# One prefix-sum matmul per unit instead of two, with exps of both signs and r divided by w, in a new order of instructions

## The chip, the cores and the metric

The kernel runs on one core of a Trainium2 chip. Its time is the device time of one execution in microseconds (us). Each run of a changed kernel is timed beside the kernel before on the same chip. A ratio is the mean time of one kernel's fast runs over the mean of the other's fast runs of the same rounds, so it is not quite the ratio of the medians that I quote; the brackets behind it are its 95% interval. One per cent is 2.2 us here. A single profiled execution can be a microsecond off its kernel's median, so I take verdicts from ratios and read mechanisms from profiles.

## The reference

An RWKV-style recurrence over 4 x 768 tokens with 8 heads of 48 gives x; a gated MLP of width 1536 follows.

```python
for t in range(S):                                  # recurrence, per batch and head
    cur = einsum('bhd,bhe->bhde', u * kt, vt)
    y[:, :, t] = einsum('bhd,bhde->bhe', rt, state + cur)
    state = wt[..., None] * state + einsum('bhd,bhe->bhde', kt, vt)
xn = x / sqrt(mean(x * x) + 1e-6) * rms_g           # then the MLP on 3072 tokens
g = xn @ w_gate
out = (g * sigmoid(g) * (xn @ w_val)) @ w_out
```

## The kernel before

The tokens are cut into six super-blocks (SB0 to SB5) of 128 steps, each with four units, one per batch. A unit (m, j) needs the decay up to each step: prefix sums of ln w over the 128 steps, their exp, and r and k multiplied by it. One sum must include the step itself and the other must not, so the kernel before makes two sums with two masks, each in its own PSUM bank, and takes one exp over both banks:

```python
def cs_mm(self, m, j):                              # TensorE: the prefix sums
    ps = self.b2(("cs", m, j))                      # a pair of the 8 PSUM banks
    rhs = self.lw[:, self.slot["lw", m], j, :, 0:D]
    for i, mask in ((0, self.mask_nge), (1, self.mask_gt)):
        if i or m not in ONE_SUM:                   # ONE_SUM = () before
            self.nc.tensor.matmul(ps[:, i, 0:DM]..., lhsT=mask, rhs=rhs, start=True, stop=True)

def cs_exp(self, m, j):                             # ScalarE: in place, in the banks
    ps = self.b2(("cs", m, j))[:, :, 0:DM]
    if m in ONE_SUM:
        self.nc.scalar.activation(out=ps[:, 0], in_=ps[:, 1], func=AF.Exp, scale=-1.0)
        self.nc.scalar.activation(out=ps[:, 1], in_=ps[:, 1], func=AF.Exp)
    else:
        self.nc.scalar.activation(out=ps, in_=ps, func=AF.Exp)

def rk_mul(self, m, j):                             # VectorE: the decay product
    self.nc.vector.tensor_tensor(out=self.rkA[...], in0=self.in_rk[:, self.slot["in_rk", m], j],
                                 in1=ps_of_unit, op=ALU.mult)      # (cut) frees the bank pair
```

I call `rk_mul` the decay product. It is the last reader of the pair of banks, so until it has run no matmul can write there. That makes a chain for each super-block: ln, sums, exp, decay product, and only then the next use of those two banks, which may be another unit's sum or a gate matmul of the MLP.

All instructions are issued in an order written as a list of steps, with the engine where there is a choice (`A` ScalarE, `V` VectorE, `G` GpSimd) and after `@` the bank or the semaphore group:

```
ln.3.0.4   ln w of SB3        cs.3.1  sums of unit 1     exp.3.1  their exp     rk.3.1  decay product
ruk1.3.1   r*k on GpSimd      xn.2.1/V  normalise a tile of x     gv.2.0.3.g  gate matmul of the MLP
```

## Time and profile before

| | |
|---|---|
| time | 217.6 us median of three (216.13 to 219.59) |
| TensorE busy | 194.1 of 216.3 us, 90% |
| first gate matmul of SB0 / SB1 / SB2 | 32.91 / 66.92 / 103.35 us |
| end | 216.3 us |

The first gate matmul of a super-block's MLP is a good milestone, as the recurrence of that block must be done by then. The lines themselves are shown in the prediction.

### The profile page before, as it was taken

How to read it: one execution, taken by the hardware profiler on the slowest of the kernel's cores; microseconds unless marked ns; L12 is line 12 of the kernel's file. 1: busy time of each engine (PE TensorE's matmuls, PEld its weight loads, DVE VectorE, ACT ScalarE, POOL GpSimd, SP SyncE). 2: the span in 40 equal slices, each digit the busy share in tenths (PEclk: the TensorE clock that was granted, in tenths of full speed). 3: DMA queues.
4: the chain of work that ended last, by engine and by line, in shares of the span. 5: the costliest groups of instructions: out<-in, count | busy, mean ns of one | idle time of the engine just before them, and what ended most of it. 6: DMA issues, size and time to landing. Idle time of an engine off the chain costs nothing.

```text
span 216.3 us, 4472 instructions
## 1 busy us (share of the span) xinstructions
PE 194.1 (90%) x1660; PEld 119.0 (55%) x1660; DVE 151.8 (70%) x244; ACT 128.1 (59%) x232; POOL 111.4 (52%) x139
## 2 busy tenths in 40 slices
PE   1257999999899999886999999999999999999992
PEld 0035547887577868663345555455564555544451
DVE  2039678084999989989779969798968995226530
ACT  3355895668967896586434777637986426034401
POOL 3277895058766969495951662776966012000000
PEclk9999999999999999999699999999999999999999
DMA  6999979999999899999999798999557512221013
GB/s 138 185 213 260 364 258 295 314 189 217 188 220 196 180 179 228 141 207 148 220 195 209 142 240 171 165 211 223 128 124 161 41 54 41 65 99 72 5 36 109
DMA packets 130774, 36.94 MB, mean 171 GB/s; under 512 B 124480, under 2 KB 129216, under 8 KB 130752
## 3 DMA queue, kind: packets, MB, share of 16 engines
q1 hardware_dynamic: 130352, 36.65, 78.8%
q8 instruction: 13, 0.21, 0.4%
q14 instruction: 9, 0.07, 0.2%
q10 hardware_dynamic: 400, 0.00, 0.1%
HBM read 26.15 MB, written 4.72 MB: 143 GB/s over the span
## 4 chain that ended last, share of the span: by engine, by line
PE 67%; SPq 8%; POOL 8%; DMA 5%; issue 4%; ACT 4%; DVE 2%; ACTq 0%; POOLq 0%; DVEq 0%
PE ps L511 37%; PE ps L527 16%; SPq L290 7%; PE ps L498 4%; PE ps L411 2%; PE ps L370 2%; DMA rkT<-rkA 2%; PE ps L427 2%; DMA xnt<-xnr 2%; POOL st L446 1%; POOL ydr L464 1%; PE ps L399 1%; POOL ruk L452 1%; DVE rkA L386 1%; PE ps L424 1%
## 5 line engine op out<-in xcount | busy, mean ns | idle before, releaser
L515 ACT ACTIVATE sg<-ps 128x512 bf16<-128x512 f32 x72 | 41.4, 596 | 37.4 <-PE ps L511 30.3
L519 DVE TENSOR_TENSOR ht<-ps,sg 128x512 bf16<-128x512 f32 x72 | 48.0, 685 | 18.4 <-PE ps L511 12.1
L511 PE MATMUL ps<-xnt,wg 128*128 128x256 bf16 (+1 forms) x288 | 56.3, 330 | 0.9 <-DVE xnt L335 0.5
L511 PE MATMUL ps<-xnt,wv 128*128 128x256 bf16 (+1 forms) x288 | 55.7, 329 | 0.0
L527 PE MATMUL ps<-wo,ht 128*128 128x384 bf16 x288 | 53.5, 326 | 0.0
L511 PEld LDWEIGHTS <-wv 128*128 128x128 bf16 x288 | 27.9, 99 | 18.2 <-issue 1.4
L527 PEld LDWEIGHTS <-ht 128*128 128x128 bf16 x288 | 27.3, 98 | 18.0 <-DVE ht L519 0.2
L452 POOL TENSOR_TENSOR ruk<-in_rk 128x384 f32<-128x384 f32 x24 | 24.6, 1028 | 23.5 <-DMA in_rk<-in_r_dram 13.5
L511 PEld LDWEIGHTS <-wg 128*128 128x128 bf16 x288 | 27.1, 98 | 17.2 <-issue 1.9
L414 DVE TENSOR_TENSOR qts<-ps,mask_lt 128x1024 bf16<-128x1024 f32 x24 | 28.7, 1217 | 2.0 <-PE ps L411 1.9
L477 POOL TENSOR_TENSOR rstd<-rstd,mhalf 128x1 f32<-128x1 f32 x24 | 13.5, 565 | 26.9 <-ACT junk L472 26.8
L386 DVE TENSOR_TENSOR rkA<-in_rk,ps 128x768 bf16<-128x768 f32 x24 | 22.5, 949 | 5.7 <-ACT wcr L363 2.2
L456 POOL TENSOR_TENSOR ruk<-ruk,u_bc 128x384 f32<-128x384 f32 x24 | 24.4, 1023 | 2.0 <-DMA u_bc<-in_u_dram 1.3
L379 ACT ACTIVATE ps<-ps 128x768 f32<-128x768 f32 x24 | 18.6, 795 | 9.0 <-PE ps L370 8.4
L464 POOL TENSOR_TENSOR ydr<-in_v,diag 128x384 f32<-128x384 f32 x24 | 20.3, 850 | 4.3 <-DVE diag L459 4.2
L472 ACT ACTIVATE junk<-xb 128x388 bf16<-128x388 bf16 x24 | 12.6, 524 | 12.9 <-DVE xb L468 12.8
L370 PE MATMUL ps<-lw,mask_nge 128*128 128x384 bf16 x24 | 8.5, 354 | 11.3 <-ACT lw L329 8.4
L459 DVE TENSOR_REDUCE diag<-ruk 128x8 f32<-128x384 f32 x24 | 13.0, 544 | 4.4 <-POOL ruk L456 4.4
L326 ACT ACT_TABLE_LOAD x12 | 15.4, 1283 | 0.9 <-PEq L571 0.7
L446 POOL TENSOR_TENSOR st<-sf,wcr 128x384 bf16<-128x384 f32 x17 | 14.0, 828 | 2.3 <-ACT wcr L363 2.2
L339 ACT COPY obr<-ps 128x384 f32<-128x384 f32 x14 | 6.6, 478 | 12.6 <-PE ps L527 12.4
L468 DVE TENSOR_TENSOR xb<-ps,ydr 128x384 bf16<-128x384 f32 x24 | 12.9, 549 | 1.6 <-PE ps L427 1.6
(71 smaller groups left out, 201.8 us busy)
## 6 DMA issues: line engine op xcount, KB each, us to landing
in_w<-in_w_dram SPq DMA_DIRECT2D x24, 192.0 KB, 3.7
in_rk<-in_k_dram SPq DMA_DIRECT2D x24, 192.0 KB, 3.8
in_rk<-in_r_dram SPq DMA_DIRECT2D x24, 192.0 KB, 4.1
in_v<-in_v_dram SPq DMA_DIRECT2D x24, 192.0 KB, 3.9
out_dram<-obr SPq DMA_DIRECT2D x24, 192.0 KB, 2.1
ht<-in_moe_w_val_dram SPq DMA_DIRECT2D x4, 384.0 KB, 4.3
ht<-in_moe_w_out_dram SPq DMA_DIRECT2D x4, 384.0 KB, 6.3
ht<-in_moe_w_gate_dram SPq DMA_DIRECT2D x3, 384.0 KB, 8.2
```

The lines of the kernel that those rows point to most:

```text
L326: self.nc.scalar.preload_act_table_set(LN_EXP if kind == "le" else SILU)
L379: self.nc.scalar.activation(out=ps, in_=ps, func=AF.Exp)
L386: self.nc.vector.tensor_tensor(out=self.rkA[:, self.slot["rkA", m, j], :, :, 0:D], in0=self.in_rk[:, self.slot["in_rk", m], j], in1=self.b ...
L414: self.nc.vector.tensor_tensor(out=self.qts[:, self.slot["qts", m, j]].rearrange("p a q t -> p (a q) t"), in0=self.b2(("qb", m, j)).rearra ...
L446: (self.nc.vector if eng == "DVE" else self.nc.gpsimd).tensor_tensor(out=self.st[:, m % 2, j].rearrange("p q (a d) -> p q a d", a=2), in0= ...
L452: self.nc.gpsimd.tensor_tensor(out=self.ruk[:, self.slot["ruk", m, j]], in0=rk[:, 0], in1=rk[:, 1], op=ALU.mult)
L456: self.nc.gpsimd.tensor_tensor(out=t, in0=t, in1=self.u_bc, op=ALU.mult)
L464: self.nc.gpsimd.tensor_tensor(out=self.ydr[:, self.slot["ydr", m, j]], in0=self.in_v[:, self.slot["in_v", m], j], in1=self.diag[:, m * SB ...
L511: self.nc.tensor.matmul(ps[:, a * n:(a + 1) * n], lhsT=w[:, c, f * 128:(f + 1) * 128], rhs=x[:, c], start=(a == 0 and c == 0), stop=(a == ...
L515: self.nc.scalar.activation(out=self.sg[:, self.slot["sg", m, g, i]], in_=self.b1(("gvb", m, g, i, "g")), func=AF.Silu)
L519: self.nc.vector.tensor_tensor(out=self.ht[:, self.slot["ht", m], fs[0]:fs[-1] + 1, t0:t0 + n], in0=self.b1(("gvb", m, g, i, "v")).rearran ...
L527: self.nc.tensor.matmul(ps, lhsT=self.ht[:, self.slot["ht", m], f, j * L:(j + 1) * L], rhs=self.wo[:, f, :], start=(f == 0), stop=(f == FC ...
```

## The change

The intent is to take one of the two prefix-sum matmuls away in the 16 units of SB2 to SB5. One sum stays, and its exp is taken with both signs. What the second sum had more, the step's own ln w, is put back by multiplying r with exp(-ln w). The order of instructions was then searched anew, and it differs nearly everywhere.

```diff
-ONE_SUM = ()
+ONE_SUM = (2, 3, 4, 5)
+    def inv_w(self, m):                    # ScalarE, once per super-block: 1/w = exp(-ln w)
+        self.nc.scalar.activation(out=self.iw[...], in_=self.lw[...], func=AF.Exp, scale=-1.0)
-    def r_over_w(self, m, j):              # was there, unused
+    def r_over_w(self, m, j, eng):
         r = self.in_rk[:, self.slot["in_rk", m], j, 0]
-        self.nc.gpsimd.tensor_tensor(out=r, in0=r, in1=self.in_w[...], op=ALU.divide)
+        (self.nc.vector if eng == "DVE" else self.nc.gpsimd).tensor_tensor(
+            out=r, in0=r, in1=self.iw[...], op=ALU.mult)
 # the order, a piece at the end of SB3's recurrence (all of it changed)
-... xn.2.1@1/V exp.3.1 o.1.3.2 dm.3.1/G vc.3.0.4@1/V xd.2.1 cs.3.2@3 exp.3.0 ruk2.3.1 o.1.2.2 rk.3.1@0 ...
+... rw.3.1/V rw.3.0/G cs.3.1@0 o.1.3.1 vc.3.0.4@1/V exp.3.0 xd.2.3 rs.2.1 o.1.3.2 xn.2.1@0/G dke.3@0 rw.3.2/V
+exp.3.1 o.1.2.2 ruk2.3.2 rk.3.0@1 ...
```

`iw` is the new exp for 1/w, `rw` the multiplication of r by it. Eight of the 16 `rw` are on VectorE and eight on GpSimd. Of the 24 normalisations 16 are on GpSimd, where it had 4.

## The prediction

> **What bounds the kernel now.** I read the page first (engines, slices, groups), then the windows view for three stretches that I chose, then the timeline of TensorE around the one hole in it. The page says that TensorE is busy for 90% of the span, far more than any other engine, and that its granted clock dips once, in the 20th slice:
>
> ```profile
> PE 194.1 (90%) x1660; PEld 119.0 (55%) x1660; DVE 151.8 (70%) x244; ACT 128.1 (59%) x232; POOL 111.4 (52%) x139
> ...
> PE   1257999999899999886999999999999999999992
> ...
> DVE  2039678084999989989779969798968995226530
> ...
> PEclk9999999999999999999699999999999999999999
> ```
>
> The averages hide three stages, so I cut the span at 33 us (the first gate matmul starts) and at 103.35 us (the first gate matmul of SB2 starts). The columns are the stretch, its length, and the busy time of TensorE, its weight loads, VectorE, ScalarE and GpSimd, then granted clock, DMA share and GB/s:
>
> ```profile
> core 0: us, PE busy (x) PEld busy (x) DVE busy (x) ACT busy (x) POOL busy (x), PEclk, DMA share, GB/s
> 50.00:103.35 53.35, 48.36 (x562) 36.13 (x561) 48.33 (x71) 40.86 (x74) 40.20 (x46) 1.00 1.03 190
> 103.35:212.50 109.15, 108.44 (x792) 57.48 (x792) 76.90 (x120) 56.25 (x104) 43.31 (x54) 0.98 0.62 130
> 0.00:33.00 33.00, 20.33 (x158) 11.07 (x159) 16.65 (x34) 19.38 (x33) 21.33 (x32) 1.00 0.93 236
> ```
>
> What the reader is to see: from 103.35 to 212.5 us TensorE is busy for 108.44 of 109.15 us, so in this late stage each matmul taken away is time taken away. From 50 to 103.35 us TensorE and VectorE are level (48.4 and 48.3 of 53.35 us, 91% each), so VectorE is a second bound there. In the head TensorE works 20.3 of 33 us, and 31 of its 36 warm-up matmuls are in that; loads and casts rule it. The last piece, 212.5 to 216.3, is an eviction and a store, which the change does not touch.
>
> The middle stage ends in a hole (start, duration, then the group, with the idle time ahead of it in brackets):
>
> ```profile
> 99.28 0.81 PE L527 MATMUL ps<-wo,ht 128*128 128x384 bf16 x4
> 101.81 0.32 PE L370 MATMUL ps<-lw,mask_nge 128*128 128x384 bf16 x1 [1.72 <-DVE rkA L386]
> 101.97 0.32 PE L370 MATMUL ps<-lw,mask_gt 128*128 128x384 bf16 x1
> 102.14 0.33 PE L435 MATMUL ps<-vb,rkA 128*128 128x96 bf16 x4
> 102.68 0.34 PE L435 MATMUL ps<-vb,rkA 128*128 128x96 bf16 x4 [0.21 <-DVE rkA L386]
> 103.35 1.20 PE L511 MATMUL ps<-xnt,wg 128*128 128x512 bf16 x3 [0.33 <-DMA xnt<-xnr]
> 104.34 1.49 PE L511 MATMUL ps<-xnt,wv 128*128 128x512 bf16 x3
> ```
>
> TensorE idles 2.3 us in these lines. The chain of waits goes back from 103.35 through a 3.6 us transposing DMA to a run of GpSimd work from 79.4 to 99.1 us (with one 2.8 us hole), so the new x tiles of SB2 come late. Three 512-column matmuls take 1.2 to 1.5 us here against 0.81 later: the clock is down until about 107.6 us.
>
> **What the Trainium skill says.** "TensorE: Matmul & The Clock Gate", section "Wait — 56ns, not 53.3ns?": warm matmuls start N / 2.4 GHz plus about 2.5 ns apart, 162.5 ns for 384 columns. The trace agrees: the two above start 101.97 - 101.81 = 0.16 us apart. So the mean of 354 ns in the row for this matmul is mostly pipeline latency that overlaps, and a removed one is worth 0.163 us and not 0.354. The same page, "What's actually happening", says that the clock halves after an idle window of about 3.4 us; the dip after the hole fits that kind of thing, though the idle time seen is shorter. "ScalarE: Activation LUTs", "What ACT_TABLE_LOAD costs": 186 ns plus 0.833 ns per element with constant scale. The trace's exp of 768 columns (795 ns) and ln of 1536 (1476 ns) are within 5% of it, and exp and ln share one table set here. "SBUF — State Buffer", "Who interferes with whom": a VectorE tensor_tensor with both inputs in SBUF contends with GpSimd's reads. This trace's case of it, the state decay on VectorE, took 1.05 us at 85.07 (GpSimd working) and 0.55 us at 131.92 (GpSimd idle).
>
> ```profile
> L379 ACT ACTIVATE ps<-ps 128x768 f32<-128x768 f32 x24 | 18.6, 795 | 9.0 <-PE ps L370 8.4
> L329 ACT ACTIVATE lw<-in_w 128x1536 bf16<-128x1536 f32 x4 | 5.9, 1476 | 0.2 <-issue 0.2
> L345 POOL TENSOR_SCALAR xnr<-xb,rstd 128x384 bf16<-128x384 bf16 x4 | 5.0, 1251 | 0.3
> L446 DVE TENSOR_TENSOR st<-sf,wcr 128x384 bf16<-128x384 f32 x3 | 2.2, 721 | 0.0
> ```
>
> **The change, part by part.** *TensorE.* 16 units (SB2 to SB5, four each) lose one 384-column matmul: 16 x 0.163 = -2.6 us. By the order of instructions SB2's and SB3's eight come before the first gate matmul of SB2, SB4's and SB5's eight after it: -1.3 us in the middle stage, -1.3 us in the late one. Nothing else in its work changes; both orders have 36 warm-ups.
>
> *ScalarE.* One exp of 768 becomes two of 384: an estimate of 795 - 384 x 0.833 = 475 ns each, so 2 x 475 - 795 = +0.155 us, 16 times: +2.5. Four exps of 1536 for 1/w: 4 x 1.476 = +5.9. The new order gives it five fewer normalisations (-3.0 at 607 ns) and five more output evictions (+2.4 at 478 ns), and shifts about -2 of small copies. Sum some +6, 128 to 134 us.
>
> *VectorE.* Eight of the 16 multiplications r x (1/w): fp32, both inputs in SBUF, 384 columns, the form of the decay row: 8 x 0.72 = +5.8. Seven fewer normalisations at 502 ns are -3.5, five fewer evictions at 552 ns -2.8, and it gets two more small copies of several kinds, about +1.5. Sum +1, about 153 us.
>
> *GpSimd.* The other eight multiplications at the 1.03 us of its fp32 products: +8.2. Normalisations rise from 4 to 16: 12 x 1.25 = +15. Sum +23, 111 to about 134 us.
>
> What lies beside other work: in the late stage the extra 2.5 + 3.0 of ScalarE, and all of GpSimd's, which is busy for 43 of 109 us there. On the path: the eight matmuls of the late stage, -1.3 us, the one part that I call certain. In the middle stage the additions fall on full engines. By 103 us VectorE has to do five multiplications (+3.6) for two normalisations (-1.0) and two evictions (-1.1) less and two small copies more (+0.7): +2.2, 48.3 to 50.5 of 53.35 us. GpSimd gets two multiplications (+2.1) and four normalisations (+5.0): 40.2 to about 47.3. ScalarE gets two exps of 1.48 and eight times 0.155: about +4. The saving of 1.3 on TensorE is there met by +2.2 on VectorE, and the last normalisation before the late stage moves from VectorE (0.5 us) to GpSimd (1.25 us), on the chain that ends the stage. I put the middle stage at +0.5 us, between -3 (the hole closes and the clock stays up) and +3.
>
> The head is ordered anew: a gate weight is loaded first of all, and gate weights for the first block are asked for earlier. Up to the first gate matmul the new order has 26 warm-ups before it and not 31. As loads set the head, I give that -1 us, between -3 and +2.
>
> Sum: -1.3 + 0.5 - 1.0 = -1.8; with a little for a new search over the rest, -2.1: 217.6 - 2.1 = 215.5 us.
>
> **The rivals.** First, the order finds a way to keep TensorE full in the middle too: then -2.6, and of the 2.3 us hole and the slow clock behind it (12 matmuls of 512 columns from 103.35 to 107.62 us, which at 0.216 us would take 2.6: 1.7 us lost) most comes back: 217.6 - 2.6 - 3 - 1 = 211. For it speaks that the order was searched for this very set of durations; against it that every other engine gets fuller just where the hole is. Second, VectorE or GpSimd becomes the bound of the middle stage: +2.2 to +3.5 us there, -1.3 later, head even: 219. For it speaks the 91% of VectorE and that each step waits in order behind others; against it that 53.35 us still exceeds both sums. Third, the products of VectorE and GpSimd hinder each other: five products at 1.05 and not 0.72 us would add 1.7 us, inside the range. A DMA rival I think weak: bytes and transposes are the same, and the share falls to 0.62 in the late stage.
>
> **Range and chances.** The parts' limits (middle -3 to +3, head -3 to +2) are not all met at once; I take 212.0 to 218.8 us as the range for 8 in 10. Faster by over 2% means below 213.2: it needs the first rival nearly whole, 0.22. Slower by over 2% means above 222: 0.04. Within: 0.74.
>
> **What would show it.** In the windows, 0.16 us per removed matmul and a late stage of 107 to 108 us. Two exps per unit at about 475 ns, the exp for 1/w at 1.48, the products at 0.55 to 1.05 us on VectorE and about 1.0 on GpSimd. In the middle stage VectorE over 93% and GpSimd near 90%, with a hole of a microsecond or more and a clock dip before the first gate matmul of SB2. I am wrong if that hole and dip are gone, if new holes of over 1 us stand in the late stage, or if the head moves by over 3 us.

## The result, and the profile after

The changed kernel is slower: its ratio to the kernel before is 1.0365 [1.0271, 1.0459]. Its two fast runs took 224.34 and 225.1 us, two slow ones 229.85 and 232.42 (left out), against a median of 217.14 us before. The result is correct. The profiled run is a fast one with a span of 223.2 us, 6.9 more than before.

From the page of the changed kernel, engines and slices:

```profile
PE 192.4 (86%) x1644; PEld 116.6 (52%) x1644; DVE 157.2 (70%) x245; ACT 132.6 (59%) x248; POOL 135.6 (61%) x158
...
PE   0449678999898987976799998899999999999993
...
POOL 3157995553499999699956599706989335200000
PEclk9976999999999999999589999999999999999999
```

GpSimd gained 24 us where +23 was foreseen, 9 of them in the first half of the span: there its row is nearly all nines from the 12th to the 20th slice, where TensorE's row is now broken. The windows of the changed kernel, cut at its own first gate matmuls of SB2 and SB0 (columns as in the prediction):

```profile
core 0: us, PE busy (x) PEld busy (x) DVE busy (x) ACT busy (x) POOL busy (x), PEclk, DMA share, GB/s
50.00:109.36 59.36, 50.12 (x571) 37.27 (x568) 52.82 (x81) 46.02 (x83) 49.84 (x54) 0.97 0.84 171
109.36:219.69 110.33, 108.29 (x780) 56.48 (x779) 77.25 (x114) 58.82 (x114) 55.71 (x63) 0.98 0.58 126
0.00:30.41 30.41, 15.94 (x120) 8.39 (x121) 14.39 (x28) 14.17 (x24) 17.99 (x29) 0.89 1.01 243
```

What the reader is to see: the first gate matmul of SB0 comes 2.5 us earlier, the middle stage is 6.0 us longer, and the late stage 1.2 us longer although eight of its matmuls are gone; TensorE's idle time in it rose from 0.71 to 2.04 us. In the middle stage no engine is at its limit by the sums: TensorE 84%, VectorE 89%, GpSimd 84%. All of them wait more.

The head is not really shorter. In the new order the first gate matmuls are a lone group of six; warm-ups and the recurrence follow, and the next gate group starts at 36.04 us (34.87 before). I added up the TensorE work that was left at 50 us in both profiles, without warm-ups, each matmul at the prediction's N / 2.4 GHz + 2.5 ns: 152.5 us before and 151.6 in the changed kernel. The change takes 2.6 us away, all of it later, so the changed kernel was an estimated 1.7 us behind at 50 us. Of the 6.0 us, 1.7 are thus work that the head left over.

Where they wait is seen at the end of SB3's recurrence, just ahead of the first gate matmul of SB2. This is the timeline of the changed kernel there (start, duration, engine, then in brackets the idle time ahead of it and what ended it):

```profile
99.98 1.47 ACT L388 ACTIVATE iw<-lw 128x1536 f32<-128x1536 bf16 x1
...
101.56 2.44 POOL L351 TENSOR_SCALAR xnr<-xb,rstd 128x384 bf16<-128x384 bf16 x1
...
102.88 0.86 DVE L393 TENSOR_TENSOR in_rk<-in_rk,iw 128x384 f32<-128x384 f32 x1
...
103.97 0.99 POOL L393 TENSOR_TENSOR in_rk<-in_rk,iw 128x384 f32<-128x384 f32 x1
...
104.99 0.95 DVE L397 TENSOR_TENSOR rkA<-in_rk,ps 128x768 bf16<-128x768 f32 x1 [1.25 <-POOL in_rk L393]
...
106.00 0.32 PE L376 MATMUL ps<-lw,mask_gt 128*128 128x384 bf16 x1 [1.98 <-DVE rkA L397]
...
106.36 0.47 ACT L382 ACTIVATE ps<-ps 128x384 f32<-128x384 f32 x1 [2.23 <-PE ps L376]
106.75 0.47 ACT L383 ACTIVATE ps<-ps 128x384 f32<-128x384 f32 x1
...
107.32 0.48 PE L376 MATMUL ps<-lw,mask_gt 128*128 128x384 bf16 x1 [1.00 <-DVE rkA L397]
```

Read it downwards. ScalarE makes 1/w; GpSimd is held by a normalisation of 2.44 us and comes to its multiplication of r only at 103.97; VectorE stands idle for 1.25 us because its decay product needs that r; TensorE stands idle for 1.98 us because the decay product frees the banks of its next sum. ScalarE then waits for that sum, and so on into a second hole. Before, the same place had one hole of 1.72 us and no GpSimd product in the chain.

The new and moved groups of the changed kernel, with busy time and mean ns of one:

```profile
L382 ACT ACTIVATE ps<-ps 128x384 f32<-128x384 f32 x16 | 7.6, 478 | 4.5 <-PE ps L376 4.3
L388 ACT ACTIVATE iw<-lw 128x1536 f32<-128x1536 bf16 x4 | 5.9, 1476 | 0.1
L393 POOL TENSOR_TENSOR in_rk<-in_rk,iw 128x384 f32<-128x384 f32 x8 | 9.1, 1149 | 0.7 <-ACT iw L388 0.6
L393 DVE TENSOR_TENSOR in_rk<-in_rk,iw 128x384 f32<-128x384 f32 x8 | 6.9, 873 | 0.1
L351 POOL TENSOR_SCALAR xnr<-xb,rstd 128x384 bf16<-128x384 bf16 x16 | 21.2, 1324 | 1.1
```

So the pieces were priced about right: exps 478 ns (475 predicted), 1/w 1476, products 873 and 1149 (720 and 1030 predicted). The error is not in what the pieces cost, but in what they hold up.

### The profile page after: what moved, and what is told of

It reads as the page before. It is cut to its first block, busy times and chain, and to the rows that moved or that the text cites. A ratio compares the mean times of both kernels' runs of the same rounds, so it can differ in the third digit from the quotient of the medians.

```text
span 223.2 us, 4489 instructions
## 1 busy us (share of the span) xinstructions
PE 192.4 (86%) x1644; PEld 116.6 (52%) x1644; DVE 157.2 (70%) x245; ACT 132.6 (59%) x248; POOL 135.6 (61%) x158
## 4 chain that ended last, share of the span: by engine, by line
PE 37%; POOL 29%; SPq 11%; issue 9%; DMA 7%; DVE 4%; ACT 1%; POOLq 0%; DVEq 0%; ACTq 0%
PE ps L522 25%; PE ps L538 10%; SPq L296 8%; POOL xnr L351 7%; POOL ruk L463 5%; POOL ruk L467 5%; DMA in_rk<-in_k_dram 4%; POOL rstd L488 4%; POOL ydr L475 3%; POOL st L457 2%; POOL in_rk L393 2%; SPq L314 1%; DMA in_rk<-in_r_dram 1%; DMA xnt<-xnr 1%; DVE qts L425 1%
## 5 line engine op out<-in xcount | busy, mean ns | idle before, releaser
L526 ACT ACTIVATE sg<-ps 128x512 bf16<-128x512 f32 x72 | 42.0, 596 | 45.9 <-PE ps L522 33.5
L538 PE MATMUL ps<-wo,ht 128*128 128x384 bf16 x288 | 52.2, 326 | 0.6 <-DVE rkA L397 0.6
L522 PEld LDWEIGHTS <-wg 128*128 128x128 bf16 x288 | 27.7, 99 | 19.1 <-issue 3.1
L522 PEld LDWEIGHTS <-wv 128*128 128x128 bf16 x288 | 27.0, 98 | 18.7 <-issue 1.9
L467 POOL TENSOR_TENSOR ruk<-ruk,u_bc 128x384 f32<-128x384 f32 x24 | 23.9, 999 | 3.2 <-DMA u_bc<-in_u_dram 2.7
L488 POOL TENSOR_TENSOR rstd<-rstd,mhalf 128x1 f32<-128x1 f32 x24 | 14.4, 602 | 18.4 <-ACT junk L483 14.5
L351 POOL TENSOR_SCALAR xnr<-xb,rstd 128x384 bf16<-128x384 bf16 x16 | 21.2, 1324 | 1.1
L457 POOL TENSOR_TENSOR st<-sf,wcr 128x384 bf16<-128x384 f32 x17 | 15.0, 897 | 3.1 <-ACT wcr L369 3.1
L345 ACT COPY obr<-ps 128x384 f32<-128x384 f32 x19 | 8.9, 481 | 7.3 <-PE ps L538 6.9
L335 ACT ACTIVATE lw<-in_w 128x384 bf16<-128x384 f32 (+1 forms) x12 | 9.9, 839 | 4.5 <-DMA in_w<-in_w_dram 4.5
```

The costliest lines, as they stand in the source:

```text
L351: (self.nc.vector if eng == "DVE" else self.nc.gpsimd).tensor_scalar(out=out, in0=in_, scalar1=scale, scalar2=None, op0=ALU.mult)
L457: (self.nc.vector if eng == "DVE" else self.nc.gpsimd).tensor_tensor(out=self.st[:, m % 2, j].rearrange("p q (a d) -> p q a d", a=2), in0= ...
L467: self.nc.gpsimd.tensor_tensor(out=t, in0=t, in1=self.u_bc, op=ALU.mult)
L488: self.nc.gpsimd.tensor_tensor(out=t[:, 1:2], in0=t[:, 0:1], in1=self.mhalf, op=ALU.pow)
L522: self.nc.tensor.matmul(ps[:, a * n:(a + 1) * n], lhsT=w[:, c, f * 128:(f + 1) * 128], rhs=x[:, c], start=(a == 0 and c == 0), stop=(a == ...
L526: self.nc.scalar.activation(out=self.sg[:, self.slot["sg", m, g, i]], in_=self.b1(("gvb", m, g, i, "g")), func=AF.Silu)
```

## The experiments

Two theories from the result. One: the new work keeps engines busy (GpSimd with normalisations, VectorE and GpSimd with products), and the fuller engine sets the time. Two: the new work stands in the chain that frees the banks, so the waits grow whatever the shares are. Beside them: is it the arithmetic at all, or the order? In the old order only 14 of the 16 units can be converted, as units (3,3) and (4,1) read r for `ruk1` after their decay product. The recorded expectations number the theories otherwise: 1 is the normalisations on GpSimd, 2 the additions of the arithmetic, 3 the head and its loads, 4 the chain. Several kernels below give a wrong result on purpose: they leave out 1/w, the product or both, so as to price each.

### The order and the arithmetic apart

**Normalisations back** on the engines they had before, all else as in the changed kernel.

```diff
-xn.2.2@1/G ... xn.2.3@2/G ... xn.2.1@0/G
+xn.2.2@1/G ... xn.2.3@2/G ... xn.2.1@0/V          # 24 such steps, 4 on GpSimd as before
```

> The changed kernel, order and arithmetic kept, but all 24 normalisations back on the engines that the kernel before gave them (4 on GpSimd instead of 16). Theory 1, GpSimd is overloaded between 60 and 110 us because the new order put 12 more normalisations of 1.3 us on it: the first gate matmul of SB2 comes 4 to 6 us earlier than the changed kernel's 109.4 us, and the time falls to 219 to 222 us. Theory 2, the new arithmetic (products and inverse on full engines) does it: under 2 us earlier, 224 us or more. Theory 3, head and order of loads: no change.

Measured: 224.01 us, 1.0329 [1.0288, 1.0371]. That is 0.4% below the changed kernel and inside its interval, so the normalisations aren't the main cause (the two intervals leave room for some 1.4% at most; the first gate matmul of SB2 came at 109.60 us, no earlier than 109.36). They did fill GpSimd: it was busy for 19.46 of the 20 us from 60 to 80 us in the changed kernel (14.57 before), and 18.21 here. But at the end of SB3's recurrence, TensorE of this kernel now waits longer:

```profile
106.56 0.48 PE L373 MATMUL ps<-lw,mask_gt 128*128 128x384 bf16 x1 [4.81 <-DVE rkA L394]
107.88 0.48 PE L373 MATMUL ps<-lw,mask_gt 128*128 128x384 bf16 x1 [0.84 <-DVE rkA L394]
```

The time that TensorE won ahead of the hole is in the hole.

**The new order with two sums**, and without 1/w and products: the old arithmetic, result correct.

```diff
-ONE_SUM = (2, 3, 4, 5)
+ONE_SUM = ()                                       # and all iw and rw steps taken out
```

> The new order, engines and head kept, but the old arithmetic: two prefix-sum matmuls in every unit, no inverse, no product. TensorE gets its 2.6 us back. Theory 1 (normalisations on GpSimd): still slow, 222 to 227 us. Theory 2 (the arithmetic's own additions to VectorE, GpSimd and ScalarE): 217 to 220 us in spite of the added matmuls. Theory 3 (head and loads of the new order): 225 us or more.

Measured: 222.27 us, 1.0269 [1.0237, 1.0302]. The order with its choice of engines, at the old arithmetic, costs 2.7% or 5.8 us. The page has, for each run, the chain of work that ended last, with the share of each engine. First the kernel before, then this run:

```profile
PE 67%; SPq 8%; POOL 8%; DMA 5%; issue 4%; ACT 4%; DVE 2%; ACTq 0%; POOLq 0%; DVEq 0%
```

```profile
PE 49%; POOL 21%; issue 10%; SPq 7%; DVE 5%; DMA 4%; ACT 2%; POOLq 0%; DVEq 0%; ACTq 0%
```

GpSimd's share goes from 8 to 21% (29% in the changed kernel). In this run the chain lies on GpSimd's queue, but for pauses of 2.3 us at most, from 75.3 to 107.6 us; before it did so from 79.4 to 99.1. The profile infers this chain, and no run shows that GpSimd's queue sets the time: it is where to look first for the order's cost.

**The old order with one sum** in the 14 units, full arithmetic, result correct: `iw` right behind `ln`, `rw` just ahead of the unit's exp.

```diff
-ln.3.0.4@1 ... xn.2.1@1/V exp.3.1 ... cs.3.2@3 exp.3.0 ...
+ln.3.0.4@1 iw.3@0 ... xn.2.1@1/V rw.3.1/V exp.3.1 ... cs.3.2@3 rw.3.0/G exp.3.0 ...
```

> The kernel before in its old order and engines, with one prefix sum in 14 of the 16 units (two units whose product of r and k comes too late in the old order keep two sums), the inverse right behind each SB's logarithm and each product of r on the engine that the changed kernel gives it, just ahead of that unit's exp. TensorE loses 14 x 0.163 = 2.3 us. Theory 1: about 216 us, since GpSimd gets only some 8 us. Theory 2: 219 us or more, with the hole ahead of SB2's first gate matmul grown by 2 us or more. Theory 3: 215 to 216 us.

Measured: 221.94 us, 1.0248 [1.0214, 1.0281]. The arithmetic alone costs 2.5% in the old order. Two lines of its timeline, ahead of the same gate matmul:

```profile
100.63 1.34 DVE L390 TENSOR_TENSOR in_rk<-in_rk,iw 128x384 f32<-128x384 f32 x1
...
104.56 0.48 PE L373 MATMUL ps<-lw,mask_nge 128*128 128x384 bf16 x1 [4.12 <-DVE rkA L394]
```

The hole is 4.12 us where it was 1.72.

**The new order with the bare single sum**, no 1/w, no products (wrong on purpose).

```diff
 ONE_SUM = (2, 3, 4, 5)                             # all iw and rw steps taken out
```

> Wrong result on purpose: the new order and engines, one prefix sum in 16 units, no inverse, no products. Against the new order with two sums (222.3 us) it shows what the removed matmuls alone are worth there: 2.6 us if they lie on the path (219.7 us), under 1 us if the waits for VectorE and GpSimd set the time.

Measured: 222.39 us (one of four runs slow), 1.0195 [1.011, 1.0279]. Against 1.0269 with two sums, the 16 removed matmuls give some 0.7% here, and 1/w and products then take 1.7% back. Both differences are of intervals that touch, from runs on different chips, so their sizes are rough.

**The old head**: the kernel before's order up to the last gate matmul of SB0, then the new order; once with the full new arithmetic, once with two sums. Both are correct.

```diff
-tab.le.0 ldw.4.g@0 ld.0.0.r@0 ...                  # the new head
+tab.le.0 ld.0.3.w@0 ld.0.0.k@0 ...                 # the old one
```

> The kernel before's order up to the last gate matmul of SB0, then the changed kernel's order with its full arithmetic; result correct. If the new order's head costs the 1.9 us that the record of remaining TensorE work shows, this is about 2 us faster than the changed kernel: ratio near 1.027. If the head was only a shift that the middle stage swallows anyway, it stays at 1.036.

> The same with two prefix sums and without 1/w and the products (the kernel before's arithmetic); result correct. It leaves the new order of the rest alone as the only change. If head and rest share the 1.0269 of the whole new order as 1.9 to 3.9 us, ratio near 1.018. If the head alone is to blame, 1.00 to 1.005; if the rest alone, 1.027.

Measured: 225.25 us (one of four runs slow), 1.0324 [1.0251, 1.0397], and 221.7 us, 1.0168 [1.0106, 1.023]. So the head has a part of the order's cost, some 1% with two sums (2.69 against 1.68%, on two chips) and not resolved with the full arithmetic, and most of it lies behind the head. The milestones say where. This table is worked out from the profiles: start to first gate matmul of SB0, from there to the first gate matmul of SB2, from there to the end.

| us | head | SB0 to SB2 | SB2 to end |
|---|---|---|---|
| before | 32.9 | 70.4 | 112.9 |
| old order, bare single sum | 32.2 | 70.1 | 112.9 |
| old order, full arithmetic | 31.8 | 74.4 | 113.3 |
| new order, two sums | 30.6 | 75.8 | 113.6 |
| old head, new rest, two sums | 32.8 | 75.3 | 112.0 |
| old head, new rest, full arithmetic | 32.4 | 77.1 | 113.1 |
| changed kernel | 30.4 | 78.9 | 113.9 |

Nearly all of the loss is between SB0's and SB2's first gate matmuls, and order and arithmetic both put their share there. The first column flatters the new head, as said above: its lag is counted in the second. Alone, order and arithmetic cost 2.7 and 2.5%, together 3.65%, so they share a part of the waits.

### What the removed matmuls are worth

**The bare single sum in the old order** (wrong on purpose: no 1/w, no products), 14 units.

```diff
-ONE_SUM = ()
+ONE_SUM = ((2, 0), (2, 1), (2, 2), (2, 3), (3, 0), (3, 1), (3, 2), (4, 0), ...)     # 14 units, nothing else
```

> Wrong result on purpose: the old order with one prefix sum in 14 units as in the third run, but without the inverse and without the products (r stays undivided). What is left of the change is the removed matmul (-2.3 us) and an exp in two halves (+0.155 us each on ScalarE). Theory 4, the chain: between a logarithm and the product of the fourth unit with its decay, TensorE has only the output matmuls of the SB before to do and the PSUM banks are held, so the inverse and the products lie on its path: then this is 2 to 3 us faster than the kernel before, 214 to 215 us, and 7 us faster than the third run. Rival, the two exps in place of one hold the banks longer: 217 us or more.

Measured: 217.64 us, 1.0013 [0.9978, 1.0048]. Nothing, where 14 x 0.163 = 2.3 us were to be won. Its hole ahead of the SB2 gate matmul:

```profile
101.18 0.32 PE L372 MATMUL ps<-lw,mask_nge 128*128 128x384 bf16 x1 [3.03 <-DVE rkA L393]
```

Before it was 1.72: it grew by 1.31 us, and the seven matmuls taken out ahead of it are 7 x 0.163 = 1.14. Measured from the first gate matmul of SB0, the sum that ends the hole starts at 101.18 - 32.24 = 68.94 us here and at 101.81 - 32.91 = 68.90 before: the same time. TensorE gets to the wait sooner and stays there longer.

**Split exps only**: two sums, old order, the exp of 768 columns taken as two of 384 in the same 14 units, result correct. This asks whether the longer exps ate the gain.

```diff
-self.nc.scalar.activation(out=ps, in_=ps, func=AF.Exp)
+self.nc.scalar.activation(out=ps[:, 0], in_=ps[:, 0], func=AF.Exp)
+self.nc.scalar.activation(out=ps[:, 1], in_=ps[:, 1], func=AF.Exp)
```

> The kernel before, with its two sums and its order, the exp of 768 columns taken as two of 384 in 14 units; result correct. The bare single sum in this order gained nothing (1.0013) where fourteen removed matmuls were to give 2.3 us. If the split exps (0.155 us more each, between the sums and the release of their banks) ate that, this is slower by 1.5 to 2.3 us: ratio 1.007 to 1.011. If the removed matmuls were worth nothing because they lay in a wait, 1.000 to 1.003.

Measured: 217.76 us, 0.9998 [0.997, 1.0026]. The split costs nothing that can be seen. The prediction's +0.155 us per pair was also too much: in the lines above the two exps start at 106.36 and 106.75 and end by 107.22, so the pair takes 0.86 us against 0.80 for one, the two overlapping by 0.08 us. The Trainium skill has this, in "ScalarE: Activation LUTs", "What ACT_TABLE_LOAD costs" (back-to-back activations overlap by about 93 ns), and I had added the two durations without it.

**The late stage alone**: the bare single sum in the seven units of SB4 and SB5, old order (wrong on purpose). It tests the one term that the prediction called certain.

```diff
-ONE_SUM = ()
+ONE_SUM = ((4, 0), (4, 2), (4, 3), (5, 0), (5, 1), (5, 2), (5, 3))
```

> WRONG result on purpose. The kernel before's order, one sum in seven units of SB4 and SB5, without 1/w and without the products. It tests the one part of the prediction called certain: that a matmul removed in the late stage is 0.163 us of the time. If it is, 1.14 us less: ratio 0.995. If the wait for the exp and the decay product takes its place, 0.999 to 1.002. The same units with 1/w and products gave 1.0077, so their share is the difference.

Measured: 217.09 us, 0.9985 [0.9959, 1.0012]. The full value, 0.995, is just outside; no value at all is inside. At most some three quarters of a matmul's 0.163 us is gained here, and the middle of the interval is under a third. One place where the time goes is SB4's sums, first in the kernel before, then here:

```profile
131.19 0.32 PE L370 MATMUL ps<-lw,mask_nge 128*128 128x384 bf16 x1 [0.40 <-DVE rkA L386]
```

```profile
131.93 0.32 PE L372 MATMUL ps<-lw,mask_gt 128*128 128x384 bf16 x1 [1.08 <-DVE rkA L393]
```

TensorE's wait for the decay product grew from 0.40 to 1.08 us.

**The same seven units with the full arithmetic**, products on GpSimd, which is less than half busy there; result correct.

```diff
-ln.5.0.4@1 o.3.0.1 ... exp.5.3 ... exp.5.1
+ln.5.0.4@1 iw.5@0 o.3.0.1 ... rw.5.3/G exp.5.3 ... rw.5.1/G exp.5.1
```

> The kernel before in its old order with one prefix sum in seven units of SB4 and SB5 only, products on GpSimd, where TensorE is busy for 108.4 of 109.2 us and GpSimd for 43. All three theories say that the additions are hidden there: 7 x 0.163 = 1.1 us off, some 216 us. If the longer way from logarithm to exp (one inverse of 1.48 us) shows, the time is unchanged or 1 us longer.

Measured: 218.1 us, 1.0077 [1.0041, 1.0113]. So 1/w and products cost 0.9% over the bare form, 2 us (the two ran on different chips), on engines that have room. Its timeline in the late stage:

```profile
155.69 1.49 ACT L385 ACTIVATE iw<-lw 128x1536 f32<-128x1536 bf16 x1
157.26 1.95 POOL L390 TENSOR_TENSOR in_rk<-in_rk,iw 128x384 f32<-128x384 f32 x2 [0.39 <-ACT iw L385]
...
160.93 2.26 POOL L390 TENSOR_TENSOR in_rk<-in_rk,iw 128x384 f32<-128x384 f32 x2
...
163.23 0.95 DVE L394 TENSOR_TENSOR rkA<-in_rk,ps 128x768 bf16<-128x768 f32 x1 [0.89 <-POOL in_rk L390]
...
164.24 0.59 PE L519 MATMUL ps<-xnt,wg 128*128 128x512 bf16 x2 [0.96 <-DVE rkA L394]
```

GpSimd waits for 1/w, VectorE for GpSimd, and a gate matmul for VectorE, 0.96 us that the kernel before doesn't have there.

### Work, or wait?

In the old order, on top of the bare single sum (1.0013), three kernels were to split the cost of the arithmetic, all wrong on purpose: the 1/w alone; the products alone, by u in place of 1/w; and the products written to a tile that nobody reads.

```diff
 # the 1/w alone: iw steps in, no rw
+ln.3.0.4@1 iw.3@0
 # the products alone: rw steps in, no iw
-            out=r, in0=r, in1=self.iw[:, self.slot["iw", m], j], op=ALU.mult)
+            out=r, in0=r, in1=self.u_bc, op=ALU.mult)
 # the same, written aside
+            out=self.iw[:, 0, j], in0=r, in1=self.u_bc, op=ALU.mult)
```

> Wrong result on purpose: the inverse behind each logarithm, and no product. The inverse (1.48 us) delays the exps behind it on ScalarE: theory 4 says up to 1.48 us at each of the four hand-overs where it is not hidden, 216 to 220 us. If ScalarE has room there, as for the run without either, 214 to 215 us.

> Wrong result on purpose: as the run before, with the products (times u instead of 1/w, so that they wait for no inverse) and without the inverse. If the products as work and as a link ahead of the decay product cost most, 218 to 221 us; if the wait for the inverse costs most, 215 to 217 us.

> WRONG result on purpose. The old order with the bare single sum and the same 14 products (times u, no 1/w) at the same places on the same engines, but written to a tile that nobody reads, so that the decay product need not wait for them. With products read by the decay product the ratio was 1.0188, without products 1.0013. If the cost is the wait of the decay product for a product on GpSimd, this is near 1.002 to 1.008 (the products on VectorE still stand ahead of the decay product in the same queue). If the cost is the work itself on two full engines, it stays at 1.015 to 1.019.

Measured: 1/w alone 219.93 us, 1.0108 [1.0053, 1.0162]; products 222.08 us, 1.0188 [1.0107, 1.0268]; written aside 218.88 us, 1.0059 [1.0038, 1.0081]. The last came from another chip than the one before it, and its profile fell in a slow run, so I ran both side by side:

> WRONG result on purpose. The product times u again, read by the decay product, now beside its form written aside on one chip. If the wait is the cost: 1.015 to 1.02, about 1.3% over the form written aside. If the difference between the two earlier runs was one between chips, the two are within 0.3% of each other.

> WRONG result on purpose. The product written aside again, on the same chip as the form that is read. If the wait is the cost: 1.004 to 1.008, and its trace has the decay products of SB3 and SB5 no longer behind a GpSimd product. If not, the same ratio as the form that is read.

Measured: products read 221.17 us, 1.0153 [1.0105, 1.0201]; written aside 219.57 us, 1.0101 [1.0052, 1.015]. The difference is 0.5%, under what I expected, and the intervals overlap. Over the bare form the products cost 1.4 to 1.75%, and written aside 0.5 to 0.9%. So work and wait both have a part, and the ratios don't fix the split. The two profiles of this call show where each has it. Up to the first gate matmul of SB2 they are level (105.42 and 105.34 us) with the same hole of 4.08 us: there a product on VectorE stands ahead of the decay product in VectorE's own queue, and delays it whether or not it is read (read from the queue, not tested apart). The 1.0 us between their spans (218.4 and 217.4) comes in the late stage, where the form that is read has this, and the other has not:

```profile
165.57 0.95 DVE L394 TENSOR_TENSOR rkA<-in_rk,ps 128x768 bf16<-128x768 f32 x1 [0.89 <-POOL in_rk L390]
...
166.58 0.81 PE L519 MATMUL ps<-xnt,wg 128*128 128x512 bf16 x3 [0.68 <-DVE rkA L394]
```

**The products earlier in the order**, behind `ruk1` and up to 12 steps ahead of the ln (wrong on purpose).

```diff
-xn.2.1@1/V rw.3.1/V exp.3.1 ... rw.3.0/G exp.3.0
+rs.2.2 rw.3.0/G rw.3.1/V o.1.2.0@7 ... ln.3.0.4@1 ... xn.2.1@1/V exp.3.1 ... exp.3.0
```

> WRONG result on purpose. The same 14 products, read by the decay product, but put earlier in the order: right behind the multiplication by u that reads the same r, up to 12 steps ahead of the ln. Most of them are then done before the sums are; unit (2,2), whose r is read late, is not earlier. If the place on the hand-over is what costs, most of the 1.0188 goes: 1.003 to 1.010. If the work is, it stays at 1.015 to 1.019.

Measured: 224.94 us, 1.0362 [1.0303, 1.0421]. A clear miss: earlier is twice as bad. The products now stand ahead of the products of the MLP (`ht`) in the same queue, and TensorE waits for those too, while 2.83 us of the old hole (4.09 with the products in their first place) remain. First VectorE of this kernel, then its TensorE:

```profile
73.56 2.62 DVE L390 TENSOR_TENSOR in_rk<-in_rk,u_bc 128x384 f32<-128x384 f32 x2
76.11 0.68 DVE L527 TENSOR_TENSOR ht<-ps,sg 128x512 bf16<-128x512 f32 x1
```

```profile
77.90 0.50 PE L535 MATMUL ps<-wo,ht 128*128 128x384 bf16 x2 [2.06 <-DVE ht L527]
```

Two products of 0.56 us at their fastest took 2.62 us here. At the one earlier place that I tried, what is off one chain is on another.

**The clock, a rival that no run was made for.** Behind its holes ahead of SB2, the changed kernel's TensorE was granted half its clock from 106.4 to 113.2 us, the kernel before's from 103.6 to 107.0. That can't be the order's cost: with two sums in the new order the clock stayed at 1.00 there, and that is 2.7% slower. Nor does the kernel before gain when its slow stretch is absent: over all calls, 56 fast runs with a mean clock of 0.996 or more took 217.42 us on average, 50 with less 217.34. What the longer stretch costs the changed kernel is not shown; it lies partly in the late stage, but costs that stage only an estimated 0.2 us more than before (half of 3.84 against half of 3.4 us).

No kernel tried beats the kernel before. The nearest correct ones are the split exps (0.9998) and the late stage alone (1.0077).

## Why the prediction was wrong

It said 215.5 us, at most 218.8, and gave slower by over 2% a chance of 0.04. It came out 3.65% slower.

- **The step that failed first: "in this late stage each matmul taken away is time taken away", -1.3 us, "the one part that I call certain".** The late stage got 1.2 us longer (109.15 to 110.33). Taken alone, seven of these matmuls gave 0.15% where 0.5% was due, and with 1/w and products the same units cost 0.8%. TensorE's 108.44 of 109.15 us was read rightly as full, but full of work in an order. What the runs show in its place: at a hand-over TensorE waits for a decay product to free the banks, and with sums taken out it waits longer (0.40 to 1.08 us at SB4's sums). That all of the missing gain goes there isn't shown.
- **The term that was mis-sized most: the middle stage, put at +0.5 us, between -3 and +3.** It measured +6.0 by the prediction's own cuts, of which an estimated 1.7 were left over by the head. Its inputs in this stage were near: VectorE 52.8 us where 50.5 was put, GpSimd 49.8 for 47.3, ScalarE 46.0 for 45. What failed is the rule made of them, in the second rival: "against it that 53.35 us still exceeds both sums". The sums did fit into the stage; 1/w, product and decay product come one after another ahead of the bank release and don't share the time with each other.
- **The removed matmuls of the middle stage** were worth -1.3 in the sum and nothing on the chip: the bare form gave 1.0013, its hole took up the time to within 0.2 us.
- **The order.** "For it speaks that the order was searched for this very set of durations" was an argument of the first rival, and "a little for a new search over the rest" was -0.3 us. The order alone measured +5.8 us. The head's term had the wrong sign: the first gate matmul of SB0 came 2.5 us earlier, where -1.0 was put, but it is a lone group, and by SB1's the changed kernel was 2.8 us behind (69.76 against 66.92 us). My windows ended the head at 33 us and began the middle at 50; that stretch had no window and no term.
- **The rivals.** The second, VectorE or GpSimd as the bound of the middle stage, 219 us, had the direction and the place; GpSimd was busy for 19.46 of 20 us from 60 to 80 us. But it was meant as a sum of busy time, and moving the normalisations back gained 0.4%, which can't be told from nothing. The third, products that hinder each other, is seen: 873 ns on VectorE for 720, from 547 to 1346. It is worth 8 x 0.15 = 1.2 us of busy time. VectorE's whole sum was put at +1 and came to +5.4 us (151.8 to 157.2), with the small copies at some +3.9 where +1.5 was put.
- **"What would show it"** held for the durations of the pieces and for the hole and the clock dip ahead of SB2's gate matmul; VectorE was at 89% there and not over 93, GpSimd at 84% and not near 90, the late stage 110.3 us and not 107 to 108. None of the three signs of being wrong appeared: hole and dip stayed, the longest hole of the late stage was 0.62 us, and the first gate matmul moved by 2.5 us. They were badly chosen, as the prediction was wrong without them.

The account, rough: the order +5.8 us, the removed sums -1.6 in that order, 1/w and products +3.7; together +7.9, and 3.65% of 217.1 is 7.9. They add up by construction, each being the step from one run to the next. These are differences of ratios whose intervals touch, save for the first. What stays open is what in the new order costs its share between SB0 and SB2: head and normalisations each explain less than half of it, and I took no third part of it apart. The chain's share on GpSimd (8, 21 and 29%) is the one lead.

## What to carry to other kernels

Before a removed instruction is counted as time, look for the next wait on its engine: if that wait ends with another engine's work, the time saved goes into the wait. A new operation is priced by its place, whether it stands ahead of the one that frees a buffer, in the dependence or merely in the same in-order queue, and not by the share of its engine; and a changed order is an own change, to be run alone with the old arithmetic before anything is said about the arithmetic. Cut the profile into windows without gaps, and measure progress by the work that is left, as the first instruction of a stage can be moved ahead alone.

## What the Trainium skill lacked or had wrong

- "Perfetto Trace Analysis", "Identifying Performance Opportunities", says that improving a kernel is in general improving its most-contended engine, and its part "Identifying the Most-Contended Engine" warns that TensorE's busy share is not a good measure. Here TensorE had the highest busy share (90%), and 14 of its matmuls taken away, 2.3 us, gave 1.0013 [0.9978, 1.0048]: the warning holds (weight loads, which the page would go by, were at 55%, VectorE at 70%). The page's "Optimization Strategy", to look at the gaps and what ends them, is what pointed to the cause. It lacks a word on relieved work moving into an existing gap (1.72 to 3.03 us here).
- "SBUF — State Buffer", "Who interferes with whom", says that a VectorE tensor_tensor with both inputs in SBUF contends with GpSimd's reads. The runs agree in part, and give sizes for one form: in the changed kernel a fp32 product of 384 columns on VectorE took 1.29 and 1.35 us beside GpSimd's fp32 products of r, k and u (at 83.0 and 84.2 us), but 0.56 and 0.86 us beside a GpSimd normalisation (at 101.54 and 102.88) and 0.55 us beside a GpSimd product begun 0.1 us after it (at 164.38).
- "TensorE: Matmul & The Clock Gate", "What's actually happening", gives an idle window of about 3.4 us ahead of the slow clock. In the changed kernel TensorE was busy for 1.35 of the 3.4 us before the clock fell at 106.4 us (holes of 1.98 and 1.00 us); with two sums in the same order and no hole over 0.7 us there, it stayed at 1.00. No page gives the busy share below which such a window counts as idle.
- No page of the skill that I read tells how long a chain over ScalarE, GpSimd, VectorE and PSUM gets per added step. Here the 1/w and the products made a wait of 1.72 us one of 4.12 us.
- No page that I read has a case in which a stretch at half clock does not show in the time. Here 50 fast runs of the kernel before with a mean clock under 0.996, which the profiles have as a slow stretch of 3.4 us, took 217.34 us on average, and 56 without 217.42.
